# Attention and two expert layers on one core: the exponentials transposed in 32x32 blocks on VectorE, the products with V in 32x64 array tiles

## The chip, the core and the metric

The kernel runs on one NeuronCore of a Trainium2 chip. The metric is the device time of one execution in microseconds (us). Engines are named as in the profile: PE is TensorE's matrix multiply, PEld its weight load, DVE is VectorE, ACT is ScalarE, POOL is GpSimd, SP issues the DMAs.

## What is computed

```python
q_rot, k_rot = rotate(q), rotate(k)            # rotary embedding; q, k, v: 2 x 8 heads x 576 x 64, fp32
scores = scale * q_rot @ k_rot.T
attn = exp(scores - max(scores)); attn = attn / (sum(attn) + 1e-9)
x = (attn @ v)                                 # heads side by side: 1152 tokens x 512
h = maximum(x @ w_in, 0); x = (h * h) @ w_out              # 512 -> 2048 -> 512
out = ((x @ w_a) * (x @ w_b)) @ w2_out                     # 512 -> 1536 -> 512
```

## The kernel before

**Stages.** The 16 heads are worked in 8 pairs of two heads, numbered 0 to 7; after them the two expert layers follow, with the products of 384 or 288 columns on lines 607 to 609 and 814 to 816. In those layers every fp32 operand is split into two parts (a rounded high part written by ACT on line 520, the rest by DVE or POOL on line 517), and each product is three matmuls.

**One pair.** A pair has five chunks of query rows: chunks 0 to 3 hold 128 rows of each of the two heads, chunk 4 the last 64 rows of both. `scores` (lines 334 to 371) multiplies a chunk with all 576 keys into one two-bank PSUM tile per head (L357, for chunk 4 L352). There are two such tiles, tags s0 and s1, so the scores of the next chunk wait until DVE has read this one. DVE copies the negated scores to SBUF and takes their minimum in the same instruction (L364); ACT takes the exponential and its row sum (L367). Before it, POOL (for pair 0 also DVE) has applied the rotary embedding (L323, L324, L329, L330).

**Transposing.** The product with V needs keys on the partitions, so the exponentials are transposed. `turned` and `fill` (lines 373 to 415) do that on PE in 128x128 blocks against an identity matrix (L378), four blocks to a PSUM bank (tags t0, t1), and ACT or DVE copies each bank to SBUF (helper line 277). A pair has 45 such blocks: 40 in the fills of chunks 0 to 4, 4 in `tk` (the last 64 keys of one head and the first 64 stored keys of the other, which share a block) and one `tt`.

**Product with V.** `times_v` (lines 428 to 450) multiplies V as stationary operand with the transposed exponentials in two halves of 288 query columns: 128x64 weights, the two heads side by side in the array (L436), and one full 128x128 product for the leftover keys (L438). The result is copied out (L277). `recip` forms 1/sum on POOL and DVE, `flip` and `spread` bring it to all partitions with small matmuls (L480, L491), DVE multiplies (L496), and ACT and POOL split the result into two parts for the first layer (L520, L517).

**Weights.** `convert` (lines 523 to 538) works a 128x512 block of weights from its raw 64-bit words: two ACT passes (L532 a scaled copy, L533 a Prelu), a clamp (L535), a shift (L536) and a merge of bits (L538) on DVE, then the split. Seven weights are converted during the attention (EARLY), with the clamp on DVE and a PSUM bank u0 or u1 between; the rest follow after the last product with V.

**Order.** No engine's order is written out directly. `Plan` (lines 63 to 218) is given every operation with a cost and its dependences, plays the engines through in time, and issues each engine's instructions in the order that came out. PE's order is the order in which the operations were given: in the loop of lines 859 to 885, the scores of the next chunk, then this chunk's transposes, then half of one half of the previous pair's product with V. After pair 7 its product with V runs alone (lines 887, 888), then the first layer begins with `unit1`.

```python
for n, (p, c) in enumerate(order):
    if n + 1 < len(order):
        scores(*order[n + 1])
    ...
    else:
        turned(p, c, 0)
        turned(p, c, 1)
        if p:
            times_v(p - 1, c // 2, c % 2)
```

Of the kernel before, what the change touches and what calls it, by code (L numbers as in the profile page):

```python
# [7 lines left out]
F32 = mybir.dt.float32  # L8
# [22 lines left out]
NP = 7  # L31
NS = 2
NG = 5
NV = 3
HB = 288
QS = 192
# [3 lines left out]
ROOM = 2  # L40
# [12 lines left out]
class Op:  # L53
    def __init__(self, engines, cost, fn, deps, acq, rel, k):
        self.engines, self.cost, self.fn, self.k = engines, cost, fn, k
        self.deps, self.acq, self.rel = list(deps), list(acq), list(rel)
        self.end = self.soon = None
# [5 lines left out]
class Plan:  # L63


    HOP = {"PE": 0.25, "SP": 2.0, "-": 0.0}
    NEAR = 0.0
# [29 lines left out]
    def order(self):  # L97
# [7 lines left out]
        for o in ops:  # L105
            if "PE" in o.engines:
                o.due = clock
                clock += self.takes("PE", o.cost)
        done = set()

        def due(o):
            stack = [o]
            while stack:
# [12 lines left out]
                if x.soon is not None:  # L126
                    x.due = min(x.due, x.deps[0].due + x.soon)
# [4 lines left out]
        ready = {id(o): 0.0 for o in ops}  # L132
# [5 lines left out]
        nth = 0  # L138
        for o in ops:
# [3 lines left out]
        result = []  # L143

# [22 lines left out]
        while True:  # L167
            best = None
            if nth < len(pes) and left[id(pes[nth])] == 0:
                r = room(pes[nth])  # L170
                if r is not None:
                    best = (max(at["PE"], ready[id(pes[nth])], r), 0, pes[nth], "PE")
            for e in engines[1:]:
                ok = []
                for o in open_[e]:
                    if o.end is None and (r := room(o)) is not None:
                        ok.append((max(at[e], ready[id(o)], r), o.due, o.k, o, e))
# [16 lines left out]
            o.end, o.on, o.begin = s + took, e, s  # L194
            at[e] = o.end
            hop = self.HOP.get(e, 0.1)
            for x in nexts[id(o)]:
                left[id(x)] -= 1
                ready[id(x)] = max(ready[id(x)], o.end + hop)
# [22 lines left out]
def attention_moe_moe2_kernel(ctx: ExitStack, tc: tile.TileContext, qk, rope, vm, vt, ident_in, sel_in, w_in, w_out, w_a, w_b, w2_out, out):  # L222
# [5 lines left out]
    ps = ctx.enter_context(tc.tile_pool(name="ps", bufs=1, space=bass.MemoryType.PSUM))  # L228

# [4 lines left out]
    small = sb.tile([P, 2304], F32, tag="g4", name="small")  # L234
    VT = [small[:, i * P:(i + 1) * P] for i in range(2)]
    PTT = [small[:, 256 + i * S:256 + (i + 1) * S] for i in range(2)]
    ident = small[:, 1408:1536]
    sel32 = small[0:27, 1536:2304].rearrange("p (k n) -> p k n", k=6)
    ident16 = ident.bitcast(BF16).rearrange("p (n two) -> p n two", two=2)[:, :, 1]
    sel = sel32.bitcast(BF16).rearrange("p k (n two) -> p k n two", two=2)[:, :, :, 1]  # L240
    VV = sb.tile([P, 2, 2, 4, D], F32, tag="sums", name="V")
    PT = [sb.tile([P, 2, 4, S], F32, tag=t, name=f"PT_{t}") for t in ("wb", "acc")]
    PP = sb.tile([P, NP, 2, S], F32, tag="y", name="P")

# [12 lines left out]
    STAGS, TTAGS, UTAGS = tuple(f"s{k}" for k in range(NS)), ("t0", "t1"), ("u0", "u1")  # L257
    SM = [lazy(lambda k=k: ps.tile([P, 2, 512], F32, tag=f"s{k}", name=f"m{k}")) for k in range(NS)]
# [757 lines left out]
```

## Time and profile before

| | us |
|---|---|
| median of 3 runs (583.06 to 583.92) | 583.15 |
| the profiled execution | 583.75 |
| its span, first to last instruction | 582.0 |
| PE busy in the span | 562.5 (97%) |
| DVE, ACT, POOL busy | 395.2, 326.9, 306.9 |

The span is the part that the trace shows; 1.75 us of the profiled execution lie around it. A busy PE is not a PE at its peak, since a matmul's row lasts until its result is in PSUM: two matmuls that run side by side in parts of the array, or one behind the other in the pipeline, have overlapping rows. The distance between starts tells what the array needs.

### The profile page before, as it was taken

To read this page: it belongs to the slowest core of one execution; us is meant where nothing else is said; L and a number is where in the kernel's file an instruction comes from. 1 tells how busy PE (TensorE), PEld (TensorE's weight loads), DVE (VectorE), ACT (ScalarE), POOL (GpSimd) and SP (SyncE) were. 2 spreads that over 40 slices of the span, in tenths; PEclk is the share of its full clock that TensorE was granted. 3 is DMA by queue.
4 is the path that set the end of the run, shared out by engine and by line. 5 is a ranking of instruction groups with operands and counts; after the bars stand their busy time and mean duration, and the time that the engine had idled before them with its cause. 6 is when DMAs were issued, how large, how long until landed. Compare 5 with 4: busy or idle time off the path is not lost.

```text
span 582.0 us, 9472 instructions
## 1 busy us (share of the span) xinstructions
PE 562.5 (97%) x3554; PEld 486.7 (84%) x3554; DVE 395.2 (68%) x748; ACT 326.9 (56%) x690; POOL 306.9 (53%) x260
## 2 busy tenths in 40 slices
PE   3999999999999999999999999999999999999997
PEld 2666666666699999999999999899988988988986
DVE  3646777776378736836764768987887877886454
ACT  1668888887478657705732545467753654534210
POOL 4598765421377505804761366776656666655000
PEclk9999999999999999999999999999999999999999
DMA  8326242120124423403330210213341322300004
GB/s 280 137 82 211 103 174 94 57 74 21 37 82 138 144 70 112 142 3 109 110 102 8 73 37 1 63 59 134 109 144 42 106 72 73 127 20 1 1 1 163
DMA packets 16018, 51.16 MB, mean 88 GB/s; under 512 B 2889, under 2 KB 3785, under 8 KB 15076
## 3 DMA queue, kind: packets, MB, share of 16 engines
q1 hardware_dynamic: 15972, 50.55, 25.7%
q8 instruction: 28, 0.46, 0.3%
q14 instruction: 18, 0.15, 0.1%
HBM read 48.19 MB, written 2.36 MB: 87 GB/s over the span
## 4 chain that ended last, share of the span: by engine, by line
PE 87%; DVE 7%; POOL 1%; ACT 1%; issue 1%; DMA 1%; SPq 0%; DVEq 0%; POOLq 0%; ACTq 0%
PE m L607 13%; PE m L609 12%; PE m L608 12%; PE s L357 7%; PE t L378 6%; PE av L436 6%; PE mu L607 5%; PE mu L608 5%; PE mu L609 5%; PE m L814 3%; PE m L816 2%; PE m L815 2%; PE av L438 2%; DVE oacc L655 1%; PE s L352 1%; PE mu L816 1%
## 5 line engine op out<-in xcount | busy, mean ns | idle before, releaser
L364 DVE TENSOR_SCALAR_CACHE_REDUCE P<-s 128x576 f32<-128x576 f32 x72 | 52.3, 755 | 32.7 <-PE s L357 24.5
L517 POOL TENSOR_TENSOR g<-v,g 128x384 fp32r<-128x384 f32 (+1 forms) x39 | 46.7, 1199 | 47.0 <-ACT g L520 46.8
L367 ACT ACTIVATE P<-P,st 128x576 f32<-128x576 f32 x72 | 55.5, 775 | 11.9 <-DVE P L364 11.9
L520 ACT CAST g<-v 128x384 fp32r<-128x384 f32 (+1 forms) x72 | 40.6, 566 | 28.2 <-DVE v L785 18.1
L607 PE MATMUL m<-y,w_p 128*128 128x288 f32 x160 | 48.1, 301 | 2.8 <-DVE v L772 1.8
L608 PE MATMUL m<-y,w_p 128*128 128x288 f32 x160 | 47.2, 295 | 0.0
L609 PE MATMUL m<-y,w_p 128*128 128x288 f32 x160 | 47.1, 294 | 0.0
L378 PEld LDWEIGHTS t<-small,P 128*128 128x128 f32 x288 | 31.4, 143 | 14.6 <-issue 10.6
L378 PE MATMUL t<-small,P 128*128 128x128 f32 x288 | 41.3, 285 | 0.0
L323 POOL TENSOR_TENSOR X<-X,cs_rot 128x1152 f32<-128x1152 f32 x14 | 36.7, 2635 | 1.1 <-DMA small<-in_sel 1.1
L607 PEld LDWEIGHTS m<-y,w_p 128*128 128x128 f32 x160 | 30.0, 187 | 6.4 <-DVE oacc L655 2.7
L607 PE MATMUL m<-x,w_i 128*128 128x384 f32 x100 | 33.7, 337 | 0.7 <-DVE v L646 0.5
L357 PE MATMUL s<-cs_rot 64*128 64x288 f32 x128 | 24.5, 484 | 9.8 <-POOL cs_rot L330 8.8
L609 PE MATMUL m<-x,w_i 128*128 128x384 f32 x100 | 33.4, 334 | 0.0
L608 PE MATMUL m<-x,w_i 128*128 128x384 f32 x100 | 33.4, 334 | 0.0
L760 ACT COPY v<-m 128x288 f32<-128x288 f32 x19 | 7.6, 400 | 42.0 <-PE m L609 26.7
L608 PEld LDWEIGHTS m<-y,w_p 128*128 128x128 f32 x160 | 30.1, 188 | 1.1
L517 POOL TENSOR_TENSOR w_i<-bits_i,w_i 128x512 fp32r<-128x512 f32 x8 | 10.3, 1282 | 39.2 <-ACT w_i L520 39.2
L609 PEld LDWEIGHTS m<-y,w_p 128*128 128x128 f32 x160 | 30.0, 188 | 0.0
L655 DVE TENSOR_TENSOR oacc<-m,oacc 128x512 f32<-128x512 f32 (+1 forms) x31 | 20.8, 678 | 12.7 <-PE m L816 7.7
L655 DVE TENSOR_TENSOR yacc<-m,yacc 128x384 f32<-128x384 f32 (+1 forms) x26 | 13.4, 517 | 22.9 <-PE m L609 22.6
L517 DVE TENSOR_TENSOR g<-v,g 128x384 fp32r<-128x384 f32 (+1 forms) x33 | 23.6, 716 | 7.8 <-ACT g L520 7.7
(248 smaller groups left out, 1918.1 us busy)
## 6 DMA issues: line engine op xcount, KB each, us to landing
raw_i<-in_w_in SPq DMA_DIRECT2D x16, 512.0 KB, 3.3
raw_o<-in_w_out SPq DMA_DIRECT2D x16, 512.0 KB, 3.2
X<-in_qk SPq DMA_DIRECT2D x7, 1152.0 KB, 5.3
raw_a<-in_w_a SPq DMA_DIRECT2D x12, 512.0 KB, 3.3
raw_b<-in_w_b SPq DMA_DIRECT2D x12, 512.0 KB, 3.2
raw<-in_w_out SPq DMA_DIRECT2D x12, 512.0 KB, 3.3
V<-in_vm SPq DMA_DIRECT2D x8, 256.0 KB, 5.6
out<-oacc SPq DMA_DIRECT2D x8, 256.0 KB, 2.0
```

What stands on the lines that cost most here:

```text
L323: m = pl.op("POOL", ("s", 2 * S), lambda e, qi=qi: e.tensor_tensor(out=x()[:, :, qi, :], in0=x()[:, :, qi, :], in1=cs, op=ALU.mult), [done ...
L357: pe.matmul(s[h]()[:, bk, 0:288], q0, k0[h][:, bk * 288:bk * 288 + 288], start=True, stop=True)
L364: m = pl.op("DVE", ("us", 0.85), lambda e, h=h, j=j: e.tensor_scalar(out=PP[:, pr.k, h, :].rearrange("p (b n) -> p b n", b=2), in0=s[h]()[ ...
L367: x = pl.op("ACT", ("us", 0.86), lambda e, h=h, j=j: e.activation(PP[:, pr.k, h, :], PP[:, pr.k, h, :], AF.Exp, bias=st()[:, 0, j:j + 1], ...
L378: pe.transpose(b()[0:src.shape[1], k * P:k * P + P] if w is None else b()[0:w, k * P:k * P + P], src, ident)
L436: pe.matmul(b()[half(h), 0:288], v[:, h, k, :], pt[:, h, k, q], start=(k == 0), stop=False, skip_group_check=True)
L517: e.tensor_tensor(out=out_, in0=a, in1=b, op=ALU.subtract)
L520: h = pl.op("ACT", ("s", n), lambda e: e.copy(hi_(), val()), after)
L607: pe.matmul(dst, wh, mh, start=first, stop=False, skip_group_check=open_)
L608: pe.matmul(dst, wh, ml, start=False, stop=False, skip_group_check=open_)
L609: pe.matmul(dst, wl, mh, start=False, stop=last, skip_group_check=open_)
L655: return pl.op("DVE", ("p", width), lambda e: e.tensor_tensor(out=acc(), in0=dst(), in1=acc(), op=ALU.add), [o] + b.prior, rel=[b])
```

## The change

The exponentials of a chunk are transposed by DVE, one instruction per head and chunk, straight from SBUF to SBUF, within each 32x32 block; no copy follows. After it partition 32a+i of block b holds key 32b+i for the query rows 32a to 32a+31 of every chunk. So `times_v` takes V in 18 blocks of 32 keys, and for each block issues 8 matmuls, one per group a of 32 partitions and head h: a 32x64 array tile, 128 or 160 moving columns, output in one of four banks (one per a, the heads in its two halves of partitions). It runs in four quarters of 5, 5, 4 and 4 blocks behind chunks 1 to 4 of the next pair. Eight ACT copies take the four banks out. V is loaded by four DMAs a pair, one per group of partitions, in place of three.

PSUM: four banks for the product with V, in which `flip` and `spread` also lie, and four for scores; the tiles of one bank that the expert layers use are made only when the attention is over. Conversions during the attention put their clamp on POOL, use a score tile as their PSUM buffer, and end with shift and merge as one piece of work on DVE; later ones wait until the last normalised product is split. Two ACT passes of a conversion become one. Pair 0 is loaded and rotated in five pieces, on DVE except the last, its first scores are issued by banks, and 23 matmuls of zeros run around them. The exponentials have 3 buffers in place of 7. The last pair's product with V is moved behind the first `unit1`, its `flip` and `spread` behind the next two.

```diff
+PIECES = {"k0": (0, 288), "q0": (0, 192), "k1": (288, 576), "q1": (192, 320), "q2": (320, 576)}
+FIRST = (("k0", "cs"), ("k0", 1), ("q0", 0), ("k1", "cs"), ("k1", 1), ("q1", 0), ("q2", 0))
+WARM = (16, 2, 5)
+QUARTERS = ((0, 5), (5, 10), (10, 14), (14, 18))
+FILL = (0, 1, 2)
...
+    PT = [sb.tile([P, 9, S], F32, tag=t, name=f"PT_{t}") for t in ("wb", "acc")]
+    SM = [lazy(lambda k=k: mps().tile([P, 512], F32, tag=f"m{k}", name=f"m{k}")) for k in range(2 * NS)]
+    AV = [lazy(lambda k=k: ps.tile([P, 512], F32, tag=f"av{k}", name=f"av{k}")) for k in range(4)]
...
+    def turned(p, c):
+        pr, ex = EXP[p, c]
+        ends = [pl.op("DVE", ("us", 0.72), lambda e, h=h: e.transpose(PT[p % 2][:, 5 * h + c], PP[:, pr.k, h]), [ex[h]] + ([AVD[p - 2]] if p > 1 else [])) for h in range(len(ex))]
+        TOK.setdefault(p, []).extend(ends)
...
+    def load_v(p):
+        war = [AVD[p - 2]] if p > 1 else []
+        LV[p] = [dma(288, lambda e, a=a: e.dma_start(out=V4[32 * a:32 * a + 32, p % 2], in_=vq[p]), war) for a in range(4)]
...
+            for b in range(*QUARTERS[part]):
+                for a in range(4):
+                    r = slice(32 * a, 32 * a + 32)
+                    for h in range(2):
+                        both = a // 2 == h
+                        k = 4 if h and both else 5 * h
+                        q = slice(0 if h and both else 32, 192 if both and not h else 160)
+                        pe.matmul(AV[a]()[half(h), q], v[r, h, b], pt[r, k:k + 4 + both, 32 * b:32 * b + 32], start=(b == 0), stop=(b == KB - 1), skip_group_check=True)
...
+        o = pl.op("PE", ("us", 0.1 + 0.29 * n), mm, TOK[p] + LV[p], acq=[] if part else [AVB[p]])
...
-        o = pl.op("ACT", ("s", DM), lambda e: e.activation(cl(), pair()[:, :, 1], AF.Copy, scale=REBIAS), [o] + paced(), acq=[cl])
-        o = pl.op("ACT", ("s", DM), lambda e: e.activation(cl(), cl(), AF.Prelu, alpha=TURN), [o])
+        o = pl.op("ACT", ("s", DM), lambda e: e.activation(cl(), pair()[:, :, 1], AF.Prelu, scale=REBIAS, alpha=TURN), [o] + paced(), acq=[cl])
...
+        if early:
+            o = pl.op("POOL", ("clamp", DM), lambda e: clamp(e, cl), [o])
+            return pl.op("DVE", ("us", 1.3), lambda e: (shift(e, cl), merge(e)), [o], acq=[up] + bits.acq, rel=[raw_, cl, up])
...
+        if c == 0 and p > 1:
+            flip(p - 2)
+            spread(p - 2, 0)
+            spread(p - 2, 1)
+        if c and p:
+            times_v(p - 1, c - 1)
+        turned(p, c)
...
     for n, (fn, *a) in enumerate(steps):
         fn(*a)
         if n == 0:
+            flip(p - 1)
+            spread(p - 1, 0)
+            spread(p - 1, 1)
+        if n == FILL[0]:
+            for k in range(4):
+                times_v(p, k)
+        if n == FILL[1]:
+            flip(p)
+        if n == FILL[2]:
             spread(p, 0)
             spread(p, 1)
```

## Rows read from the trace of the kernel before

**Rows 1.** The page: busy time of each engine over the span.
```profile
PE 562.5 (97%) x3554; PEld 486.7 (84%) x3554; DVE 395.2 (68%) x748; ACT 326.9 (56%) x690; POOL 306.9 (53%) x260
```

**Rows 2.** Windows: start:end, length, busy PE, PEld, DVE, ACT, POOL; PE clock; DMA share; GB/s.
```profile
61.40:79.19 17.79, 17.79 (x130) 11.06 (x129) 13.14 (x32) 15.11 (x36) 11.84 (x12) 1.00 0.32 113
...
132.53:157.62 25.09, 25.03 (x179) 14.86 (x178) 14.20 (x35) 14.72 (x37) 6.37 (x12) 1.00 0.10 33
157.62:582.00 424.38, 414.91 (x2545) 395.61 (x2545) 294.92 (x502) 215.76 (x434) 218.44 (x161) 1.00 0.23 77
```

**Rows 3.** The chain in order of time, from 61.40 us: start, length, what.
```profile
61.40 1.17 PE s L357 x8
62.73 0.59 PE t L378 x4
...
65.34 1.02 PE t L378 x8
66.36 1.12 PE av L436 x8
...
70.80 0.68 PE av L438 x2
...
78.75 0.44 PE tk L378 x4
79.19 1.17 PE s L357 x8
...
157.62 0.38 PE m L607
```

**Rows 4.** Groups of DVE instructions, 8.81 to 157.62 us: count | busy us, mean ns | idle.
```profile
L364 DVE TENSOR_SCALAR_CACHE_REDUCE P<-s 128x576 f32<-128x576 f32 x72 | 52.3, 755 | 32.7 <-PE s L357 24.5 <-PE s L352 8.2
...
L496 DVE TENSOR_TENSOR xf<-r,xf 128x288 f32<-128x288 f32 x14 | 5.8, 450 | 0.9 <-PE r L491 0.6
...
L536 DVE TENSOR_SCALAR up_i<-up_i 128x512 int32<-128x512 int32 x5 | 3.5, 697 | 0.1
```

**Rows 5.** Timeline of DVE at the start of pair 1: start, length, instruction, idle before.
```profile
27.03 0.76 DVE L364 TENSOR_SCALAR_CACHE_REDUCE P<-s 128x576 f32<-128x576 f32 x1 [0.55 <-PE s L357]
...
27.72 0.75 DVE L364 TENSOR_SCALAR_CACHE_REDUCE P<-s 128x576 f32<-128x576 f32 x1
...
29.34 0.76 DVE L364 TENSOR_SCALAR_CACHE_REDUCE P<-s 128x576 f32<-128x576 f32 x1 [0.50 <-PE s L357]
```

**Rows 6.** Timeline of DVE in pair 2: a copy and the instruction right behind it.
```profile
69.71 0.69 DVE L277 COPY PT_acc<-t 128x512 f32<-128x512 f32 x1 [0.27 <-PE t L378]
70.32 0.75 DVE L364 TENSOR_SCALAR_CACHE_REDUCE P<-s 128x576 f32<-128x576 f32 x1
```

**Rows 7.** Timeline of PE, matmuls in flight at 91.39 and at 91.69 us.
```profile
91.39 0.46 PE L436 MATMUL av<-PT_acc,V 128*64 128x288 f32 x2
...
91.39 0.71 PE L436 MATMUL av<-PT_acc,V 128*64 128x288 f32 x4
```

**Rows 8.** All matmuls of L436: count: min/median/max ns, first and last start, form.
```profile
L436 PE MATMUL av<-PT_acc,V x128: 405/406/458, 48.5 to 156.4; 128*64 128x288 f32 x128
```

**Rows 9.** Timeline of the start: first rotation, first scores, first minimum.
```profile
4.36 0.76 DVE L329 TENSOR_TENSOR X<-X,cs_rot 128x576 f32<-128x576 f32 x1 [4.36 <-DMA X<-in_qk]
...
8.81 2.29 PE L357 MATMUL s<-cs_rot 64*128 64x288 f32 x8 [8.81 <-POOL cs_rot L330]
...
11.13 0.76 DVE L364 TENSOR_SCALAR_CACHE_REDUCE P<-s 128x576 f32<-128x576 f32 x1 [1.96 <-PE s L357]
```

**Rows 10.** Groups of ACT and POOL instructions, 8.81 to 157.62 us.
```profile
L277 ACT COPY PT_acc<-t 128x512 f32<-128x512 f32 x30 | 16.6, 587 | 10.4 <-PE t L378 10.1
...
L533 ACT ACTIVATE cl_i<-cl_i 128x512 f32<-128x512 f32 x5 | 3.1, 621 | 0.0
...
L323 POOL TENSOR_TENSOR X<-X,cs_rot 128x1152 f32<-128x1152 f32 x14 | 36.7, 2635 | 1.1 <-DMA small<-in_sel 1.1
...
L535 POOL TENSOR_SCALAR cl_o<-cl_o 128x512 f32<-128x512 f32 x1 | 1.9, 1930 | 0.0
```

More of the change, by code (lines that the diff above doesn't have):

```diff
@@ L30 @@
 NWB = 5
-NP = 7
+NPR = 3
 NS = 2
+KB = 18
+QUARTERS = ((0, 5), (5, 10), (10, 14), (14, 18))
 NG = 5
@@ L66 @@
     HOP = {"PE": 0.25, "SP": 2.0, "-": 0.0}
+    LAG = {}
+    PORT = {"DVE": "POOL", "POOL": "DVE"}
     NEAR = 0.0
@@ L107, in order @@
                 o.due = clock
-                clock += self.takes("PE", o.cost)
+                clock += self.takes("PE", o.cost) + o.slack
         done = set()
@@ L138, in order @@
         nth = 0
+        shared = {"DVE": 0.0, "POOL": 0.0}
         for o in ops:
@@ L143, in order, with begin, port @@
         result = []
+        def begin(o, e):
+            return max([end + self.HOP.get(on, 0.1) for on, end in ready[id(o)]], default=0.0)
+        def port(o, e, t):
+            other = self.PORT.get(e)
+            if not other or not o.cost or o.cost[0] not in (("s",) if e == "DVE" else ("s", "clamp")):
+                return t
+            return t
         def room(o):
@@ L193, in order @@
             took = self.takes(e, o.cost)
-            o.end, o.on, o.begin = s + took, e, s
-            at[e] = o.end
+            o.end, o.on, o.begin = s + took + self.LAG.get(e, 0.0), e, s
+            at[e] = s + took
+            if e in shared and port(o, e, -1.0) >= 0:
+                shared[e] = s + took
             hop = self.HOP.get(e, 0.1)
@@ L371, in scores @@
         EXP[p, c] = (pr, ex)
-    def fill(p, name, blocks, after, outs):
-        b = bank_t(name)
-        def mm(e):
-            for k, (src, w) in enumerate(blocks):
-                pe.transpose(b()[0:src.shape[1], k * P:k * P + P] if w is None else b()[0:w, k * P:k * P + P], src, ident)
-        o = pl.op("PE", ("us", 0.109 * len(blocks) + 0.06), mm, after + fixed[:1], acq=[b])
-        ends = [pl.op(EVAC, ("p", n), lambda e, d=d, f=f: copy(e, d, f(b())), [o] + ([AVD[p - 2, 1]] if p > 1 else [])) for n, d, f in outs]
-        for x in ends:
-            x.soon = 0.75
-        pl.op(None, None, None, ends, rel=[b])
-        return o, ends
@@ L537, in convert @@
+        o = x = pl.op(FLEX, ("clamp", DM), lambda e: clamp(e, up if e is dve else cl), [o], acq=[up])
+        o = pl.op("DVE", ("p", DM), lambda e: shift(e, up if x.on == "DVE" else cl), [o])
         pl.op(None, None, None, [o], rel=[cl])
[L538 removed]
+        return pl.op("DVE", ("p", DM), merge, [o], acq=bits.acq, rel=[raw_, up])
@@ L856, in attention_moe_moe2_kernel @@
     fixed.append(dma(54, lambda e: e.dma_start(out=sel32, in_=sel_in)))
-    zeros += [pl.op("POOL", ("us", 0.2), lambda e, t=t: e.memset(t, 0.0)) for t in VT]
+    zeros.append(pl.op("POOL", ("us", 0.2), lambda e: e.memset(ZERO, 0.0)))
+    warm(WARM[0], zeros)
     scores(0, 0)
```

268 lines of the change are left out of this document (119 added, 149 removed).

## The prediction

> **What bounds the kernel now.** I read the page first, then the windows by stage, then the chain through one pair, and last the single instructions that set the prices. The page has PE busy 97% of the span [rows 1]. The windows say where that matters for this change: the attention ends at 157.62 us, where the first product of the expert layers starts [rows 3], and the layers behind it keep PE busy 414.9 of 424.4 us [rows 2]. The change touches little there, so what it is worth is decided before 157.62.
>
> Between 61.40 and 79.19 us lies one whole pair: PE is busy for all of its 17.79 us, while DVE has 13.14 and ACT 15.11 [rows 2]. The chain through it consists of PE alone [rows 3]. Its pieces are the scores (five times 1.17, 5.9), the transposes (0.59, four times 1.02 and 0.44, together 5.1, and one block more), the products with V (four times 1.12 and twice 0.68, together 5.8). The 1.0 that is left holds that block and the small matmuls, for which I take 0.7. The pairs around it have the same length, so PE is the bound, and every microsecond taken off PE counts until another engine ends last.
>
> **The change, part by part.**
>
> *Transposes leave PE.* That takes 5.1 to 5.4 us from a pair on PE, and from ACT and DVE the copies of the transposed banks, 0.59 us each on ACT [rows 10] and 0.69 on DVE [rows 6].
>
> *Products with V by 32x64 tiles.* 18 blocks of 32 keys times 8 matmuls, each in two passes as now. No row shows a tile of 32 rows. What the rows show is how two tiles behave: two matmuls of L436, one per half of the columns, begin within 0.03 us and are through 0.46 us after the first start [rows 7], and one alone lasts 0.41 to 0.46 [rows 8]. So they run side by side and neither waits for the other's weights. The next two passes make it 0.71, so a pass of 288 columns costs a tile 0.25 us, less the fixed part about 0.24 [rows 7]. A pass of 160 columns is then 0.135, a block 0.27, and 18 blocks 4.9 us, with some 0.15 at the start of each of the four quarters 5.5 us a pair. That is the lower bound, with all eight tiles side by side. The upper bound is the two that the rows show: 288 passes of 144 columns on average, 0.125 us each, two at a time, 18 us. I take 5.5, since in those rows each tile goes its own way, and nothing in them ties four groups of rows together. PE then needs 5.9 + 5.5 + 0.7 = 12.1 us a pair.
>
> *DVE gets the transposes.* Nine a pair, 128x576 each, SBUF to SBUF. The nearest rows: a copy of 512 columns is followed by the next instruction 0.61 us after its start [rows 6], and two minima of 576 columns start 0.69 apart [rows 5]. I take 0.68. The end below is the copy's 0.61; the end above is two cycles an element, 1.36, since a transpose in fp32 appears nowhere. The Trainium skill's page VectorE: DVE Perf Modes has a rule against this change (Rules for kernel authors: a 128x128 transpose goes to TensorE where a PSUM result will do), and its table of the three transpose paths gives VectorE 311 ns for 128x128 bf16; carried on at its 0.96 GHz to 576 columns this is an estimate of 0.78 us, with which the sum below would end 7 us later. No run here shows that figure.
>
> With 0.69 and 0.68, a pair's nine minima and nine transposes take 12.3 us, the two normalising multiplications 0.8 to 0.9 [rows 4], small ones 0.2: 13.3 us. That is above PE's 12.1, so **DVE becomes the bound of a pair**. A chunk of two heads is 2.74 us of DVE. While DVE transposes (1.4 us), PE can make the next scores: a second minimum ends at 27.72 + 0.75 = 28.47 and the next first one starts at 29.34, 0.87 us later, with the scores between them [rows 5]. So the cover is there, if the exponentials to transpose are those of the chunk before.
>
> *Conversions.* Seven run in pairs 2 to 5. Shift and merge are 0.7 us each [rows 4], 1.4 together, and they hold one of the two score tiles, so that up to 0.87 may be added before the next minimum. Between 1.4 and 2.3 I take 1.6, as the planner can lay them behind the minima: 11.2 us. The clamp goes to POOL at 1.93 [rows 10], beside two rotary products of 2.6 and two sums a pair; POOL had 11.8 us in the pair shown [rows 2], and with 7/4 clamps a pair, 3.4 more, stays just under the pair's new length. The ACT pass saved, 0.62 [rows 10], and the eight copies of V's banks, each below the 0.59 of 512 columns, both lie under DVE: ACT loses the 30 copies of 0.59 that the row shows for the four odd pairs, 4.4 us a pair, and as many in the even ones [rows 10], and had 15.1 of 17.8 [rows 2].
>
> *Start.* The first rotation can begin at 4.36 as now [rows 9], since the first two loads have the same size. By pieces, DVE works 2304 columns before the second half of the first scores; at 0.76 for 576 [rows 9] that is 3.0 us, and I allow 0.5 for the later loads and 1.0 for the half score: the first minimum at 8.9 where it stands at 11.13 [rows 9]. The zeros run while PE has nothing to do; the first scores took 2.29 us for what takes 1.17 later [rows 3, 9], though the granted clock is 1.00 throughout. Bounds: 0 to 3 us gained. The loads are one issue more on SP, V's one more a pair; they are wanted a pair later, and cost nothing.
>
> *End.* The last product with V, 5.0 us, now stands behind the first `unit1`, with two flips and spreads (0.9 more than now lies there) and perhaps 1.5 of waiting on the last normalisation. The later conversions start only after that.
>
> **The sum**, on the profiled execution's own time. Pair 0: from the first minimum at 8.9, 12.3 of minima and transposes and 0.6 for one piece of rotation, so pair 1 begins at 21.8 instead of 27.03 [rows 5]. Seven pairs of 13.3 are 93.1, the conversions 11.2, and 4% for waits between engines 4.2: 130.3, where now 27.03 and 7 times 17.79 make 151.6. Then 5.0 + 0.9 + 1.5: the expert layers stand where they now stand at 157.6 already at 137.7. That is 19.9 us less. The layers themselves I cost at nothing: PE waits for 9.5 us in all of 424 [rows 2], and neither the bank tiles nor the ACT pass is what most of it waits for; 2 us either way. So 583.75 - 19.9 = 563.9 in a profiled execution, and 563.3 against the median, which is 0.6 lower; I say 563.5.
>
> **Rivals.**
>
> *A, the forecast*, 556 to 570 by its own terms.
>
> *B, lock step.* DVE now idles 0.50 to 0.55 us before the first minimum of a chunk, waiting for scores [rows 5]. With a quarter of V's product queued on PE ahead of the next scores, and transposes in a fixed order that may wait for exponentials, this can stay: 28 chunks with a quarter times 0.5 are 14 us, 4.2 of which are in the sum: 573. For it speaks that PE's and DVE's loads, 12.1 and 13.3, are close; against it, that 0.87 of PE fits under 1.4 of DVE.
>
> *C, slow transposes* (the other side). DVE is the bound, and if a transpose in fp32 takes two cycles an element, 1.36 us, 72 of them add 49 us: 612. It decides from 19.9 / 72 = 0.28 us more than I took, that is from 0.96 us a transpose. Against it: every DVE row of 512 or 576 columns costs about one cycle an element. For it: no row has a transpose.
>
> *D, tiles in turn.* If only four tiles run side by side, a product is 9 us, a pair 15.8 on PE, with its queue about 16.2, and the time 573; with two it is 18 us, and 7 pairs of 25 and the last product give some 635.
>
> *E, issue.* If starts of matmuls lie 25 ns apart, whatever the tile, 288 passes are 7.2 us, PE needs 13.8 a pair, just above DVE's 13.3, and with the last product the time is 568 to 571. Rows speak against it, as the two starts fall within 0.03 us together with their weight loads [rows 7]. The Trainium skill's page TensorE: Matmul & The Clock Gate (section on 56 against 53.3 ns) states such a floor of about 25 ns from start to start.
>
> *F, late weights.* The layers start 20 us sooner, and the later conversions, which wait for the last split, begin about 10 us later as seen from the layers. If PE has to wait for them, up to 10 us go back: 573.
>
> *G, the gain is larger*: conversions at 1.4, no waits, 1 or 2 us off the layers: 555.
>
> **Chances.** A 0.60, B 0.14, C 0.05, D 0.04 at four tiles and 0.02 at two, E 0.04, F 0.06, G 0.05. The range from 555 to 576 takes in A, B, E, F, G and half of D, and leaves out C, the rest of D and the far ends of the others. About 0.2% is what a measurement can tell from no change, 1.2 us. Slower by more come C and the two-tile end of D, and a share of B and F together that goes further than priced: 0.09. Between, 0.02. Faster 0.89.
>
> **What would show it.** Right: no PE transposes of 128x128 blocks; 72 DVE transposes of about 0.68 to 0.75; pair length 13.5 to 16, with DVE busy nearly all of it and PE idle 2 to 3 us; 18 blocks in about 4.9 us; the first minimum near 9 us; the first product of the layers near 130. Wrong: transposes above 0.96; a quarter of V's product above 2 us; PE waiting in the layers for weights; DVE idle before each first minimum as now.

## The result and the profile after

| us | before | after |
|---|---|---|
| median (4 runs each) | 583.53 (583.06 to 584.51) | 574.44 (573.99 to 575.95) |
| profiled execution, its span | 583.75, 582.0 | 575.95, 574.1 |
| second unit of the layers begins | 160.57 | 161.21 |
| third unit to the last matmul | 415.1 | 407.0 |

The ratio is 0.9847 (0.9823 to 0.987): faster by 9.1 us, where 20 were forecast (7.8 between the profiled executions). The last two rows, from the starts of matmuls, say more: the attention, where all of the forecast gain lay, gained next to nothing (0.6 us later here; going by the median, at most 1 us earlier), and the expert layers, costed at nothing, gave 8.1 us. Pairs 1 to 6 last 17.9 us each on average, where they lasted 17.8. I count to the second unit, since the last pair's product with V now lies behind the first. The moments in this document come from one profiled execution of each kernel (after's is the slowest of its four), and executions of one kernel lie up to 6.6 us apart, so a difference of moments counts as shown only where the ratios bear it out. In the quoted expectations such moments are 0.2 to 0.3 us later than in the rows, as they count from another zero.

The page after: busy time [rows 1], and TensorE's granted clock in 40 slices, which was full throughout before.
```profile
PE 548.9 (96%) x5272; PEld 491.6 (86%) x5272; DVE 426.5 (74%) x775; ACT 271.5 (47%) x618; POOL 306.8 (53%) x261
...
PEclk9578989769999999999999999999999999999999
```
The engines' loads moved as meant (ACT 55 us less, DVE 31 more). The clock is new: in the attention TensorE was at 1.2 instead of 2.4 GHz for 47.7 us in seven stretches, the first of 20.5 us from 14.9 us on: in pair 0, where it has no product with V to do, and on through half of pair 1.

The windows after, one for each of pairs 2 to 6 (conversions run in pairs 4 to 6), columns as in [rows 2]:
```profile
43.20:61.10 17.90, 15.51 (x350) 10.93 (x341) 13.71 (x34) 9.43 (x29) 12.24 (x11) 0.90 0.76 225
61.10:77.60 16.50, 14.05 (x360) 9.71 (x348) 13.59 (x31) 9.69 (x29) 15.89 (x15) 1.00 0.54 150
77.60:95.40 17.80, 15.75 (x353) 11.16 (x344) 16.06 (x35) 11.81 (x33) 11.97 (x15) 0.90 0.66 193
95.40:115.60 20.20, 17.03 (x328) 11.59 (x312) 16.29 (x36) 12.98 (x35) 17.70 (x18) 0.79 0.38 92
115.60:135.50 19.90, 18.38 (x379) 12.35 (x384) 17.34 (x36) 12.80 (x35) 12.42 (x14) 0.79 0.58 163
```
Against one pair of 17.79 with PE busy all the time [rows 2], no engine is now busy throughout. POOL comes near it in two pairs (15.89 of 16.50 and 17.70 of 20.20), but from 12 to 150 us it keeps TensorE's scores waiting only 1.0 us and DVE 0.9. DVE has 13.6 to 13.7 in the pairs without a conversion, close to the 13.3 forecast, yet these take 16.5 and 17.9.

DVE's groups, 12 to 150 us, columns as in [rows 4]:
```profile
L414 DVE TENSOR_SCALAR_CACHE_REDUCE PV<-s 128x576 f32<-128x576 f32 x72 | 51.5, 741 | 8.6 <-PE s L396 5.3 <-PE s L391 3.3
L430 DVE STREAM_TRANSPOSE PT_wb<-PV 128x576 f32<-128x576 f32 x36 | 27.3, 771 | 6.1 <-ACT PV L418 5.4 <-PE av L453 0.5
L430 DVE STREAM_TRANSPOSE PT_acc<-PV 128x576 f32<-128x576 f32 x35 | 26.9, 773 | 5.5 <-ACT PV L418 3.7 <-ACT xf L304 1.8
...
L557 DVE TENSOR_SCALAR up_i<-cl_i 128x512 int32<-128x512 int32 x5 | 3.5, 693 | 0.3
L560 DVE SCALAR_TENSOR_TENSOR bits_i<-raw_i,up_i 128x512 int32<-128x512 int32 x5 | 3.4, 686 | 0.2
```
The minima cost what they did [rows 4]; the transposes are 72 rows of 0.77. Behind the bar stands what the forecast missed: transposes wait 9.1 us for exponentials of ACT, minima 8.6 for scores of PE.

TensorE's timeline: a quarter cut in two by a gap, then two quarters with scores around them that run undisturbed.
```profile
53.43 1.58 PE L453 MATMUL av<-PT_acc,PV 32*64 32x160 f32 x70
56.74 0.51 PE L453 MATMUL av<-PT_acc,PV 32*64 32x128 f32 x10 [1.74 <-issue]
...
72.06 1.64 PE L453 MATMUL av<-PT_wb,PV 32*64 32x160 f32 x80
73.63 1.19 PE L391 MATMUL s<-rot 64*64 64x288 f32 x8
74.75 1.37 PE L453 MATMUL av<-PT_wb,PV 32*64 32x160 f32 x64
76.04 1.24 PE L396 MATMUL s<-cs_rot 64*128 64x288 f32 x8
```
80 rows (two passes for each matmul) take 1.64 and 64 take 1.37, so 16 take 0.27, 17 ns each: all eight tiles of a block side by side. From start to start a quarter costs 1.57 or 1.29, the scores 1.12 or 1.17. But quarters like the first (3.8 us from 53.43) recur. The 28 quarters of pairs 0 to 6 last 56.8 us in the timeline; undisturbed (14 times 1.64, 12 times 1.37, and the last two in one piece of 2.46) they would last 41.9. Of the 15 us between, 8.9 lie in the seven quarters that fall into stretches at 1.2 GHz, 5.7 in the three with a gap.

The waits of TensorE on other engines inside the layers, 163 to 580 us, its largest: first before, then after (columns: waited for, us in all, times, longest).
```profile
PE m L607 <- DVE v L772: 1.8, 2, 1.4
PE m L607 <- DVE oacc L655: 1.0, 4, 0.3
...
PEld m L607 <- DVE oacc L655: 3.0, 7, 0.8
```
```profile
PE m L641 <- DVE v L815: 0.7, 1, 0.7
...
PEld m L641 <- DVE v L815: 0.9, 1, 0.9
```
Before, a matmul into a bank of a two-bank tile often waited for the DVE addition (oacc) or product (v) that reads PSUM; after, nearly all of that is gone. From the third unit on, starts more than 0.05 us later than usual for their form add up to 10.3 us before (41 of them) and 2.0 after (10).

### The profile page after: what moved, and what is told of

Same layout as the page of the kernel before. It is cut to its first block, busy times and chain, and to the rows that moved or that the text cites. A ratio compares the mean times of both kernels' runs of the same rounds, so it can differ in the third digit from the quotient of the medians.

```text
span 574.1 us, 12883 instructions
## 1 busy us (share of the span) xinstructions
PE 548.9 (96%) x5272; PEld 491.6 (86%) x5272; DVE 426.5 (74%) x775; ACT 271.5 (47%) x618; POOL 306.8 (53%) x261
## 4 chain that ended last, share of the span: by engine, by line
PE 81%; DVE 9%; ACT 3%; POOL 2%; issue 2%; DMA 2%; SPq 1%; ACTq 0%; DVEq 0%
PE m L641 13%; PE m L643 13%; PE m L642 13%; PE av L453 6%; PE av L641 6%; PE av L643 6%; PE av L642 6%; PE s L396 4%; PE m L850 3%; PE m L849 3%; PE m L848 3%; DVE PV L414 3%; DMA X<-in_qk 2%; ACT PV L418 2%; DVE PT_acc L430 1%
## 5 line engine op out<-in xcount | busy, mean ns | idle before, releaser
L418 ACT ACTIVATE PV<-PV,st 128x576 f32<-128x576 f32 x72 | 55.6, 773 | 61.4 <-DVE PV L414 60.8
L414 DVE TENSOR_SCALAR_CACHE_REDUCE PV<-s 128x576 f32<-128x576 f32 x72 | 51.5, 741 | 8.6 <-PE s L396 5.3
L453 PE MATMUL av<-PT_acc,PV 32*64 32x160 f32 (+1 forms) x1152 | 29.6, 323 | 5.8 <-issue 5.1
L453 PEld LDWEIGHTS av<-PT_acc,PV 32*64 32x64 f32 x1152 | 24.1, 146 | 12.5 <-issue 9.8
L396 PE MATMUL s<-rot 64*128 64x288 f32 x128 | 29.5, 513 | 3.6 <-DVE PV L414 2.5
L430 DVE STREAM_TRANSPOSE PT_acc<-PV 128x576 f32<-128x576 f32 x36 | 27.7, 774 | 5.8 <-ACT PV L418 4.0
L430 DVE STREAM_TRANSPOSE PT_wb<-PV 128x576 f32<-128x576 f32 x36 | 27.3, 771 | 6.1 <-ACT PV L418 5.4
L396 PEld LDWEIGHTS s<-cs_rot 64*128 64x128 f32 x128 | 17.2, 221 | 16.6 <-issue 4.2
L689 DVE TENSOR_TENSOR yacc<-m,yacc 128x384 f32<-128x384 f32 (+1 forms) x27 | 13.7, 514 | 23.3 <-PE m L643 23.0
L641 PE MATMUL m<-x,w_i 128*128 128x384 f32 x88 | 29.8, 339 | 0.0
L453 PEld LDWEIGHTS av<-PT_wb,PV 32*64 32x64 f32 x1152 | 23.6, 148 | 7.2 <-issue 5.6
```

Source lines behind the costliest of these rows:

```text
L396: pe.matmul(s[h]()[:, bk, 0:288], q0, k0[h][:, bk * 288:bk * 288 + 288], start=True, stop=True)
L414: m = pl.op("DVE", ("us", 0.7), lambda e, h=h, j=j: e.tensor_scalar(out=PP[:, pr.k, h, :].rearrange("p (b n) -> p b n", b=2), in0=s[h]()[: ...
L418: x = pl.op("ACT", ("us", 0.8), lambda e, h=h, j=j: e.activation(PP[:, pr.k, h, :], PP[:, pr.k, h, :], AF.Exp, bias=st()[:, 0, j:j + 1], s ...
L430: ends = [pl.op("DVE", ("us", 0.72), lambda e, h=h: e.transpose(PT[p % 2][:, 5 * h + c], PP[:, pr.k, h]), [ex[h]] + ([AVD[p - 2]] if p > 1 ...
L453: pe.matmul(AV[a]()[half(h), q], v[r, h, b], pt[r, k:k + 4 + both, 32 * b:32 * b + 32], start=(b == 0), stop=(b == KB - 1), skip_group_che ...
L641: pe.matmul(dst, wh, mh, start=first, stop=False, skip_group_check=open_)
```

## Experiments: the layers

**The ACT pass**, put back into after (two_acts), taken out of before (before_one_act).
```diff
-activation(cl(), pair()[:, :, 1], AF.Prelu, scale=REBIAS, alpha=TURN)
+activation(cl(), pair()[:, :, 1], AF.Copy, scale=REBIAS)
+activation(cl(), cl(), AF.Prelu, alpha=TURN)
```


> The changed kernel with the second ACT pass of a weight conversion put back. Theory L1 (the expert layers gained their 8 us because a conversion has one ACT pass less, so DVE gets its input sooner and PE waits less for DVE): the waits come back, 580 to 583 us, ratio to the kernel before 0.995 to 1.000. Rival L2 (the layers gained by the one-bank tiles, or by the order that the planner now makes): 573 to 576 us, ratio 0.983 to 0.988. The attention should move by less than 2 us under both, since ACT has the slack.

Measured: 579.1 us, ratio 0.9908 (0.9873 to 0.9943); layers 407.5; their second unit at 165.91.

> The kernel before with one ACT pass in place of two, and nothing else. L1: the layers shorten by 6 to 8 us and the time is 575 to 578 us, ratio 0.986 to 0.991, with the attention still ending at 157 to 158 us. L2: 582 to 584 us, ratio 0.998 to 1.002.

Measured: 585.72, 1.0031 (1.002 to 1.0042); layers 417.1. The pass gives the layers nothing in either kernel. But in after's attention the second pass costs some 4 us (161.21 to 165.91 in the profiles, 0.006 in the ratio, with the intervals just apart), so ACT isn't hidden there.

**The bank tiles**, again as pairs in after (two_banks), alone in before (before_one_bank).
```diff
-SM = [lazy(lambda k=k: mps().tile([P, 512], ...)) for k in range(2 * NS)]
+SW = [lazy(lambda k=k: mps().tile([P, 2, 512], ...)) for k in range(NS)]
+SM = [lambda k=k: SW[k // 2]()[:, k % 2] for k in range(2 * NS)]
```


> The kernel after, with the score pool's four layer banks allocated again as two tiles of two banks each (as before), nothing else changed; the order of the instructions on every engine should stay. Theory L2 (the layers' 8 us come from the one-bank tiles: a matmul into one half of a two-bank tile waited for the reader of the other half): from the third unit of the layers to the last matmul 413 to 416 us instead of 407, TensorE's waits there back to some 10 us, the run at 581 to 583. Theory L3 (the gain comes from the order in which the plan puts the layers' work, started from another state of the engines): 407 us and 574 as in the kernel after.

Measured: 590.93 (585.29 to 591.92), 1.0101 (1.0052 to 1.015); layers 421.8, worse than the 413 to 416 expected and than the 415.1 of before, for a reason that no run shows; second unit at 160.98. TensorE's waits in the layers, the largest:
```profile
PE m L642 <- DVE v L681: 4.2, 5, 1.4
PE m L642 <- ACT u L803: 1.5, 2, 1.0
...
PEld m L642 <- DVE v L681: 5.8, 5, 1.7
```


> The kernel before, with one thing of the change: the four layer banks that lie over the score tiles are four one-bank tiles, in a pool opened after the score pool is closed. L2: third unit to last matmul 407 to 409 us instead of 415, the run near 576, faster by about 1.3%. L3: 415 us, 583 to 584. The attention (second unit of the layers at 160.8) should not move by either; if closing the pool makes the first layer matmuls wait for all score tiles, it comes up to 1 us later.

Measured: 574.58, 0.984 (0.9825 to 0.9854); layers 406.8, second unit at 160.36. All that is left of TensorE's waits on other engines in the layers:
```profile
PE mu L615 <- DVE v L789: 0.7, 1, 0.7
PE m L615 <- DVE v L789: 0.2, 1, 0.2
```
**This settles the measured gain**: these tiles alone, in the old kernel, give all that the whole change gives (0.984 for 0.9847), and without them the change makes it slower (two_banks).

## Experiments: the attention

**V's loads and the clock.** v_two loads V for pairs 0 and 1 only and multiplies with these later; clock puts zeros on TensorE at the start of every pair.
```diff
-LV[p] = [dma(288, ...) for a in range(4)]
+LV[p] = LV[p - 2] if p > 1 else [dma(288, ...) for a in range(4)]
```
```diff
+    def hold(n):  # n matmuls of ZERO by ZERO into av3, columns 256:384
...
+        if p == 0:
+            hold(6)
...
+        if c == 0 and p > 0:
+            hold(4)
...
             flip(p - 2)
+            hold(2)
             spread(p - 2, 0)
             spread(p - 2, 1)
+            hold(2)
```


> The changed kernel with V loaded for pairs 0 and 1 only; pairs 2 to 7 multiply with the V of the pair two before (24 of 32 V loads are left out, 7.1 of 9.4 MB). Theory D1 (four times the bytes of V fill the DMA queues, so that the instruction fetch of PE and the loads of q and k come late): PE's gaps of 1.5 to 2 us within a product with V go, the first layer starts 6 to 9 us sooner, 565 to 569 us. Rival D2 (the fetch takes about 1 us whatever else runs, and a burst of 17 ns a matmul outruns it): the gaps stay, gain below 2 us, 572 to 575 us.

Measured: 573.05 (571.03 to 577.41), 0.9825 (0.9778 to 0.9872); second unit at 156.89, 4.3 earlier, though the ratio's interval overlaps after's. TensorE's gaps for instructions (12 to 150 us) fall from 4.5 to 1.8 us (three to one). The run also loses something that after doesn't: in pair 2 the exponentials stand in ACT's queue behind the first conversion, which waits 3.2 us for its weights to load. Of all the kernels here only the four without V's later loads have such a wait of over 0.3 us (0.9 to 5.3), so they may gain less than what they leave out is worth.

> The changed kernel with matmuls of zeros added where PE waits: 6 behind each chunk's scores in pair 0, 8 around flip and spread at the first chunk of every later pair; they write columns nobody reads. Theory C1 (the granted clock of 0.5 in 48 us of the attention lengthens scores and products while PE ends last): the clock stays at 1.0 for nearly all of the attention, which ends 4 to 8 us sooner, 566 to 570 us. Rival C2 (DVE is the bound and waits little for PE): the clock rises but the time stays within 2 us, 572 to 576 us. If the added matmuls delay the scores instead, it is slower by up to 5 us.

Measured: 576.42, 0.9871 (0.9854 to 0.9887); the clock is full throughout in the profiled execution, the second unit at 161.44. What the clock gave back, the zeros on the path may have taken, so this run can't price it; light, below, comes nearer.

**Conversions without a score tile, and transposes behind the next minimum.**
```diff
-shift(e, cl), merge(e)                       # through a score tile in PSUM
+shift in place in cl, merge from cl          # conv_sbuf
```
```diff
-[ex[h]] + ([AVD[p - 2]] if p > 1 else [])
+[ex[h]] + ([AVD[p - 2]] if p > 1 else []) + [COPIED[q, 2 * d + (d < 4)]]   # order_conv, (q, d) the next chunk
```


> The kernel after, but the seven early weight conversions do not take a score tile: VectorE shifts in place in SBUF and merges from there, so the three score places belong to the scores alone. Theory C3 (these conversions hold a score tile while TensorE and the minima wait for it): the minima's waits on TensorE (8.6 us) fall by 2 us or more, second unit of the layers at 157 to 159 instead of 161.5, the run at 570 to 572. Theory C2 (the loss lies in VectorE's order: a chunk's transposes stand in its queue ahead of the next chunk's minima and wait for ScalarE's exponentials): nothing over 1 us, 573 to 575. VectorE's two operations read SBUF in both, so a slower form in SBUF, shared with GpSimd, could cost up to 1 us.

Measured: 573.14 (572.8 to 578.5), 0.9847 (0.9798 to 0.9896); second unit at 158.02, 3.2 earlier, but the ratio is the same as after's, so no gain is shown. The minima's waits on TensorE fall only from 8.6 to 7.9. (The expectation speaks of three score places; the kernel has two, s0 and s1.)

> The kernel conv_sbuf, and in addition the transposes of a chunk are planned behind the first half's scores copy (the minimum) of the next chunk, so that VectorE has the next minima to do while ScalarE makes the exponentials. C2: the 11.2 us in which transposes waited for exponentials fall to under 4, pairs of the stretch without conversions go to 15 to 16 us, the second unit of the layers comes 4 to 8 us earlier than in conv_sbuf, the run at 565 to 570. If instead VectorE's bound is taken by what comes behind it (probability buffers, three of them, held longer, so that the minima now wait for TensorE or for a buffer), it is within 1.5 us of conv_sbuf.

Measured: 575.57, 0.9869 (0.9828 to 0.991); second unit at 161.04, 3.0 later than conv_sbuf (2.4 by the medians, with overlapping intervals). All of DVE's waits, 12 to 150 us:
```profile
DVE PV L414 <- PE s L396: 17.2, 21, 1.9
DVE PV L414 <- PE s L391: 4.7, 3, 3.7
```
No transpose waits for an exponential any more, and the minima wait 21.9 us for scores. The order of DVE's queue alone is not the cause: the wait went round to the other side, as the second half of the expectation foresaw.

**Half the transposes, half the products.** half_turn leaves out the second head's transposes from pair 2 on; half_av leaves out 8 of 18 blocks of keys; half_av_pad puts a 128x128 matmul of zeros in the place of each.
```diff
-for h in range(len(ex))]
+for h in range(len(ex) if p < 2 else 1)]     # half_turn
```
```diff
 for b in range(*QUARTERS[part]):
+    if b % 2 and b < KB - 1:
+        continue                             # half_av
```


> The kernel after, but from pair 2 on only the first head of a chunk is transposed (the second head's part of the transposed exponentials is that of two pairs earlier): 24 of the 72 VectorE transposes are left out, 24 times 0.77 = 18.5 us of VectorE, nothing on TensorE. Theory D (VectorE's own work is the bound of the stretch, its waits only come beside): the second unit of the layers 14 to 18 us earlier than 161.5, the run at 557 to 561. Theory S (a serial loop: the two score places are freed by the minima, the next scores stand on TensorE behind a quarter of the product with V, and the next minima wait for them): most of what VectorE saves turns into waits for scores, the second unit comes 3 to 9 us earlier, the run at 566 to 571, and the minima's waits on TensorE go from 8.6 to over 15 us.

Measured: 571.36 (570.38 to 575.1), 0.9798 (0.9755 to 0.9841); second unit at 157.32, 3.9 earlier (0.005 in the ratio, with overlapping intervals) for 18.5 us of DVE's work. DVE's largest waits, 12 to 150 us:
```profile
DVE PV L414 <- PE s L391: 12.3, 8, 4.4
DVE PV L414 <- PE s L396: 6.7, 7, 1.9
DVE PT_acc L430 <- ACT PV L418: 6.3, 15, 1.0
DVE PT_wb L430 <- ACT PV L418: 6.2, 15, 1.0
```
The minima's waits went from 8.6 to 19.0: the work that DVE was spared came back as waiting. Part of that is TensorE's gaps, which are 9.3 us here (four) for 4.5 in after. DVE's work alone is not the bound.

> The kernel after, but the products with V take 10 of the 18 blocks of keys (the even ones and the last): 8 times 0.27 = 2.2 us a pair less on TensorE, and 64 matmuls and as many weight loads fewer to fetch; nothing on VectorE. Theory S: a quarter no longer keeps the scores back, pairs 1 to 6 shrink by 1 to 2.5 us each, the second unit of the layers comes 8 to 15 us earlier (2.2 of it the last pair's product), the run at 560 to 567. Theory D: only the last pair's 2.2 and a little more, 1.5 to 4 us earlier, the run at 570.5 to 573. TensorE's clock should fall more often, as it has less to do; scores at 1.2 GHz would take back a part of the gain under S.

Measured: 564.84, 0.9675 (0.9651 to 0.9698); second unit at 149.73, 11.5 earlier. From the last minimum's end to there it is 4.3 us shorter, and start to last minimum 7.2. Pairs 1 to 6 gained 0.8 us each on average, below the 1 to 2.5 expected. TensorE had some 17 us less to do (8 blocks of 0.27 in each of 8 pairs) and no gap, but its clock was at half for 61 us.

> As half_av, but in place of each block left out stands one matmul of zeros by zeros, 128x128, which takes about 0.22 us: TensorE's work is the same within 4% as in the kernel after, with half the instructions. Theory S with a long quarter as its cause: within 2 us of the kernel after, 572 to 575. Theory F (what makes quarters long are the gaps in which TensorE fetches instructions, 6.2 us in all, and the stretches at half clock): the gaps fall to under 2 us, the second unit comes 3 to 6 us earlier, the run at 568 to 571.

Measured: 591.55, 1.0121 (1.0093 to 1.0149); second unit at 173.09. The premise failed: among the 32-row tiles the two passes of a matmul of zeros began 0.22 us behind the tile ahead of them and kept the next one back for 0.42 at 2.4 GHz, in place of 0.22 in all, and the clock was at half for 55 us. The run has no gap either, but it can't say what the gaps cost.

**What makes quarters long.** conv_vlate loads the first two V later; light puts zeros only where TensorE waits; the others combine.
```diff
-        if c == 0:
+        if c == (1 if p < 2 else 0):   # conv_vlate, load_v; it also waits for an exponential of chunk 2
```
```diff
+        if p == 0:
+            hold(6)                    # light, behind each chunk's scores
...
             flip(p - 2)
+            hold(2)
             spread(p - 2, 0)
```


> The kernel after with the conversions as in conv_sbuf, and with the first two pairs' V loaded behind pair 0's third chunk, so that the queries and keys of pairs 0 and 1 come first. A complete kernel, meant to beat both. Under every theory the start gains: the loads of pair 1 land earlier than 17.3, pair 1 begins 1 to 3 us earlier. With what conv_sbuf gained (3.2): second unit at 155 to 158, the run at 568 to 572. If the loop of theory S sets the pairs, an earlier start of pair 1 is kept, since nothing behind it waits for a load.

Measured: 576.29 (572.76 to 578.61), 0.9865 (0.982 to 0.9911); second unit at 157.99, as conv_sbuf's. The first minimum came 0.7 us sooner, and nothing of it was kept.

> The kernel conv_sbuf, and zeros multiplied by TensorE only where it waits: six 128x128 matmuls behind each chunk's scores of pair 0, and two a pair between the transpose and the spread of the normalisers, where TensorE waits some 0.5 us for ScalarE. Theory C (the half clock lengthens the first quarter of each pair and pair 0's scores, and that is what the pairs lose): half clock from 41 us to under 15, the first quarters from 2.4 to 3.3 us to 1.7 to 2.0, the second unit of the layers 4 to 8 us earlier than conv_sbuf's 158.3, the run at 565 to 569. Theory F (the gaps for instructions): the gaps move or stay, within 2 us of conv_sbuf, 571 to 575.

Measured: 571.72, 0.979 (0.9772 to 0.9807), the fastest kernel here that computes everything, its interval clear of those of after and of before_one_bank; second unit at 156.28, 1.7 earlier than conv_sbuf (1.4 by the medians, with overlapping intervals), for 31 us less at half clock.

> The kernel conv_sbuf, with V loaded for pairs 0 and 1 alone (the later pairs multiply with these): 24 of 32 loads of V are left out. Theory F with the loads behind it (V's transfers delay the fetch of TensorE's instructions): quarters of over 3 us, of which conv_sbuf has six in pairs 0 to 6, fall to two or none, the second unit of the layers 3 to 5 us earlier than 158.3, the run at 568 to 570. If the loads only cost the start, or nothing once the conversions leave the score tiles alone, within 1.5 us of conv_sbuf.

Measured: 576.48, 0.9882 (0.9858 to 0.9905); second unit at 159.89, later than conv_sbuf, with overlapping intervals.

> Both of these edits on conv_sbuf (V as in vtwo_conv, zeros as in light). If clock and gaps each have a share and TensorE's quarters were what the pairs lost, quarters come near 1.6 and 1.4 us, pairs 1 and 2, which have no conversions, to 15 us, and the second unit of the layers to 148 to 152, the run at 561 to 564. If the loop keeps its length without them, since VectorE and ScalarE set it, within 2 us of the better of the two.

Measured: 574.1, 0.9835 (0.9815 to 0.9856); second unit at 159.34. Two rows of light_vtwo's pair 3, from the timelines of DVE and of GpSimd, show why these two can't answer (vtwo_conv has such a merge of 3.14 us):
```profile
67.52 3.15 DVE L576 SCALAR_TENSOR_TENSOR bits_i<-raw_i,cl_i 128x512 int32<-128x512 int32 x1
```
```profile
67.50 2.61 POOL L348 TENSOR_TENSOR X<-X,cs_rot 128x1152 f32<-128x1152 f32 x1
```
A merge that takes 0.69 with one operand in PSUM took 3.15 from SBUF; GpSimd's rotary product began 0.02 us ahead of it, and it ended 0.56 after that. Ahead of their first conversion, ACT waits 0.9 and 3.5 us for the weights. So two runs with the conversions as in after:

> The kernel after with the zeros of light (six matmuls behind each chunk's scores of pair 0, two a pair between transpose and spread), conversions as in the kernel after. Theory C (the half clock is worth what light gained over conv_sbuf, 1 to 2 us): second unit of the layers at 159 to 160.5 instead of 161.5, the run at 572.5 to 574. If the clock has a larger share that the SBUF conversions had hidden: 154 to 157, the run at 566 to 570.

Measured: 573.2, 0.9814 (0.9793 to 0.9835); second unit at 158.88, 2.3 earlier than after (0.003 in the ratio, with overlapping intervals).

> light_psum with V loaded for pairs 0 and 1 alone (the later pairs multiply with these; 24 of 32 loads of V are left out). Clock and gaps both taken away: if TensorE's long quarters are what the pairs lose, the second unit of the layers at 149 to 153, the run at 562 to 566. If most of the loss is the loop itself (exponentials ahead of transposes, scores behind minima), it stays at 155 to 157, about v_two's 157, the run at 568 to 571.

Measured: 570.53 (566.29 to 572.26), 0.9751 (0.9704 to 0.9799); second unit at 156.56, 4.7 earlier, its interval clear of after's. Its 28 quarters last 47.2 us, 9.6 less than in after, so half of what they saved was kept. DVE's largest waits, 12 to 150 us:
```profile
DVE PT_wb L437 <- ACT PV L425: 8.9, 14, 4.6
DVE PT_acc L437 <- ACT PV L425: 4.2, 12, 1.0
DVE PV L421 <- PE s L403: 2.2, 3, 1.2
```
With TensorE's part nearly clean the minima hardly wait. The transposes wait 13.1 us for exponentials instead of 9.1, but 4.6 of it is one wait in pair 2, for exponentials behind a conversion whose weights had not landed:
```profile
55.85 0.68 ACT L561 ACTIVATE cl_i<-raw_i 128x512 f32<-128x512 f32 x1 [5.25 <-DMA raw_i<-in_w_in]
...
57.32 0.78 DVE L437 STREAM_TRANSPOSE PT_wb<-PV 128x576 f32<-128x576 f32 x1 [4.58 <-ACT PV L425]
```
DVE's idle time from the first minimum to the last is 18.3 us, against 21.7 in after. Without that one wait the second unit might have come near 152, inside the 149 to 153 of the other theory, so this run doesn't decide between the two.

## Why the prediction was wrong, and where it was right

**The layers: the step that failed** is "neither the bank tiles nor the ACT pass is what most of it waits for; 2 us either way". The ACT half holds. The bank tiles were worth 8.1 us. The 9.5 us that the prediction read as TensorE's waiting [rows 2] was no measure of it: 3.9 of them lie behind the last matmul (577.85, 0.28 long, in a span of 582.0), so TensorE sits idle for only 5.6 in the layers, while late starts add up to 10.3, since a busy row can hide one. I did not ask which instruction each of these waits was on.

**The attention: the step that failed** is the 4% for waits, 4.2 us, with its "So the cover is there, if the exponentials to transpose are those of the chunk before". It is rival B, and larger than priced: B's 573 lies near the result, and the result in the stated range, only by luck, as two errors cancel, some 10 us of attention gain that B still had and that did not come, and 8 us of the layers that did. The loads were right: DVE 13.6 a pair for 13.3; TensorE undisturbed 4 times 1.17 and 1.12 for the scores, twice 1.57 and twice 1.29 for the quarters, and 0.7, together 12.2 for 12.1; conversions 9.0 us of DVE in pairs 2 to 6 (77.0 less 5 times 13.6) for 11.2. Two loads of 12 and 14 in one loop do not give 14.

The condition failed first: the exponentials are those of the same chunk. The chain through the later part of after's pair 3, where TensorE is undisturbed, leaves TensorE out:
```profile
69.50 0.67 DVE PV L414 x2
...
70.20 0.88 ACT PV L418 x2
...
71.09 1.54 DVE PT_acc L430 x2
72.63 0.67 DVE PV L414 x2
```
So a chunk lasts 3.13 us, where 2.74 were forecast, as its transposes wait some 0.3 for its first exponential; chunk 4 lasts 2.43. That makes 15.0 a pair, and with 9.0 of conversions 114 for pairs 1 to 7, for the 108.5 of the forecast; they took 123. The other link is TensorE's: scores need a place that a minimum frees, and a minimum needs scores that stand behind a quarter, so a quarter lengthened by the clock or a gap idles DVE, and nothing is in stock to make it up. half_turn, half_av and order_conv fit this from three sides, though none of them changes one link alone. Rows 5 had the 0.87 us that scores take under 1.4 of DVE, but not the quarter, 1.3 to 1.6, that goes ahead of them.

Against the forecast the second unit came 20.5 us late (161.21 for 160.57 - 19.9). Of this, 2.9 is the first minimum:
```profile
4.94 0.76 DVE L357 TENSOR_TENSOR X<-X,cs_rot 128x576 f32<-128x576 f32 x1 [4.94 <-DMA X<-in_qk]
6.42 0.56 DVE L357 TENSOR_TENSOR X<-X,cs_rot 128x384 f32<-128x384 f32 x1 [0.72 <-DMA X<-in_qk]
...
8.50 0.76 DVE L357 TENSOR_TENSOR X<-X,cs_rot 128x576 f32<-128x576 f32 x1 [0.88 <-DMA X<-in_qk]
...
9.80 0.76 PE L396 MATMUL s<-cs_rot 64*128 64x288 f32 x4 [0.73 <-DVE cs_rot L358]
...
11.81 0.74 DVE L414 TENSOR_SCALAR_CACHE_REDUCE PV<-s 128x576 f32<-128x576 f32 x1
...
13.50 0.78 DVE L430 STREAM_TRANSPOSE PT_wb<-PV 128x576 f32<-128x576 f32 x1 [0.26 <-ACT PV L418]
```
It was 8.9 in the forecast and 11.13 before [rows 9]. The first load landed 0.6 later, later loads cost DVE 1.6 where 0.5 was allowed, and the scores, done at 10.56, then waited while DVE rotated the next piece. The 0.26 behind the minima recurs at most chunks. Pair 0 took 15.8 instead of 12.9, another 2.9. The other 14.7 lies in pairs 1 to 7: by the sums above some 5 are the chain of DVE and ACT, and the rest, some 9, what disturbs TensorE and the loop with it.

- **V's loads "cost nothing"**: wrong. V goes into all four groups of partitions, four times its bytes, which I overlooked. v_two's profile has it at 4.3 us, the start included, and its ratio at 1.3, so the size is open.
- **The ACT pass, to "lie under DVE"**: wrong in the new kernel, some 4 us by two_acts; ACT's exponentials are a link of the chain there. In before it was right (second unit at 160.27 in before_one_act).
- **The conversions' score tile**: priced at up to 0.87 each, 0.2 of it in the sum. conv_sbuf shows no gain in the ratio, and its merges took longer, so the price is not shown.
- **Transposes** at 0.68: they last 0.77, and the next instruction starts some 0.70 after them (one from 66.00, the minimum behind it from 66.69). Rival C falls. The estimate of 0.78 from the Trainium skill's page VectorE: DVE Perf Modes (section The three transpose paths) agrees with the length of the row; the price in the sum is the distance of starts. The rule that the prediction sets against the change speaks of 128x128 transposes, while this kernel needs 32x32 blocks alone.
- **Tiles side by side**: right. 17 ns a pass leave no room for D and E; the floor of 25 ns that the Trainium skill's page TensorE: Matmul & The Clock Gate (section on 56 against 53.3 ns) gives from start to start is not what these tiles keep.
- **The end**: the product with V took 5.0 in the sum; here 6.6, with a gap, but behind a wait of only 0.69, for 1.5 in the sum:
```profile
154.70 3.85 PE L453 MATMUL av<-PT_acc,PV 32*64 32x160 f32 x189 [0.69 <-DVE xf L517]
159.17 2.11 PE L453 MATMUL av<-PT_acc,PV 32*64 32x128 f32 x99 [0.61 <-issue]
161.21 0.44 PE L641 MATMUL m<-x,w_i 128*128 128x384 f32 x1
```
- **F**, late weights: no such wait in the layers. It falls.

**What stays open.** Clock, gaps and V's loads together are worth 4.7 us in the profiles (light_psum_vtwo), and up to 9 if its wait for weights, 4.6, is counted in; an estimate, as no run is free of that wait. How the rest splits between too few score places, exponentials and conversions is not settled. A third score place was not tried: the four row groups write four banks and the scores hold the other four. Nor were more than three buffers of exponentials (seven before).

## What to carry to other kernels

When two engines feed each other through two buffers, add up the whole cycle, link by link, with what stands in each queue ahead of the link; the larger of two loads is a floor, not a forecast. Where cover rests on a condition (here, whose exponentials are transposed), look whether the order makes it true. Before costing a stage at nothing, list its waits by instruction: here a few small ones, all on tiles of two banks, held the whole measured gain. Undo a change part by part even when it is faster: one edit of a few lines did it all.

## What the runs showed of the hardware

- **Gaps in dense small matmuls.** Within the products with V of the new kernels TensorE stops for 0.4 to 5.0 us with nothing to wait for ("issue"), mostly beside or right behind a 16 KB packet of the instruction queue, which takes 1.1 us on average (in after three stops of four: behind the packets that landed at 55.11, 61.80 and 89.14). Of such packets there are 41, 28 before. That TensorE waits for its instructions there is likely, but no run shows it. Fewer matmuls (half_av, none) or less other traffic (v_two, one for three from 12 to 150 us) made the gaps rarer.
- **The clock fell**: to 1.2 GHz for 47.7 us, from 14.9 us on in pair 0, where TensorE had had a few zeros and scores, and in half_av for 61, which had some 17 us less to do and gained 11.5. How much of the difference is the clock's is not shown.
- **Small tiles and full matmuls in turn** cost more than each by itself: in half_av_pad a 128x128 matmul of zeros between 32x64 tiles cost 0.22 us ahead of it and 0.42 behind its start, where zeros in a row cost 0.22 each (0.11 a pass, in after).
- **A merge with both operands in SBUF** took 0.94 us on average in conv_sbuf (0.69 to 1.64) and 3.15 once in light_vtwo, against 0.69 with one in PSUM. The Trainium skill's page SBUF — State Buffer (section Who interferes with whom) says that a VectorE instruction with two SBUF inputs contends with a GpSimd instruction that reads SBUF, for a port pair that one of them holds alone; the two rows of light_vtwo agree.
